# A float32 attention and two-layer chain on one core: the seven products of the first layer's output in another order, and two operand splits one product later

## The chip, the cores and the metric

One core of one Trainium2 chip runs the whole program in one launch. The metric is the device time of that core in microseconds (us), the median of the runs. TensorE (PE) does the matmuls, and its weight loads (PEld) overlap them; VectorE (DVE), ScalarE (ACT) and GpSimd (POOL) do the elementwise work; SyncE (SP) issues most loads. PE writes its sums into eight PSUM banks of 128 x 512 float32.

## What is computed

Attention over 2 x 8 heads, 768 positions of width 64, with a band mask and a few global keys, gives x, a matrix of 1536 x 512. Then come two gated layers:

```
a, b = x @ w1, x @ w2            # 1536 x 1024
y = ((a * b) @ w3) @ w_out       # 1536 x 512: the first layer's output
a, b = y @ w_a, y @ w_b          # 1536 x 1536
out = (a * b) @ w_out2           # 1536 x 512
```

All is float32 in the reference, so every matmul here is made of three: each operand is split into a high part (rounded for PE by a cast on ACT) and a low part (what is left, by a subtraction on DVE), and low x high, high x low and high x high are added up in one bank.

## The kernel before

**Stages.** Attention runs first, with the weight conversion and the first matmuls of layer one in its gaps. Then the gate a * b of layer one and the folded weight w3 @ w_out are finished, until about 265 us of the span. The stage of this document follows: the product y = gate x folded weight (`y_product`, lines 935 to 1007), from 265.4 to 340.4 us. Then come the products of layer two (`products`), and the output.

**Seven products for eight.** `y_product` multiplies 2 x 2 blocks with a scheme of seven products, numbered 1 to 7, where the left operand (a piece of the folded weight, tiles `wf`, or sums of pieces) and the right operand (a piece of the gate, tiles `gs`, or sums) are added beforehand and the results are combined afterwards. It does so twice: q = 0 for 1024 of the tokens (right operands 512 wide), then q = 1 for the last 512 (256 wide). A product is two halves c = 0, 1 of 128 rows; a half is 12 matmuls (four pieces of three) into one bank. So there are 14 products of 24 matmuls, 336 in all.

**Three pairs of banks.** Products 1, 6, 7 and 4 add up in the pair z, product 2 has the pair x, and products 5 and 3 share the pair m. The running sums in the banks are taken out after each product: by a copy on ACT (`nc.scalar.copy`, line 984, tiles `p` and `u`) or by an add on DVE (line 986). The next product that adds onto the same bank waits for that copy or add. The order before is 1, 2, 6, 7, 5, 3, 4:

```
for k in (1, 2, 6, 7, 5, 3, 4):
    ...
    bank = (x if k == 2 else m if k in (5, 3) else z)[c]
```

**What comes of the sums.** The finished sums are y's operands for layer two; each is split by `operand` (ACT cast at line 730, then DVE subtraction at line 731, tiles `y`). After products 2 and 5 this is emitted at once, behind the copies and adds of that product.

**The order of ACT's and DVE's work.** It is what the code emits. The generator `y_steps` (lines 791 to 924) emits the splits of the left and right operands (`left`: ACT line 808, DVE line 809; `right`: ACT line 730, DVE line 731), the sums of gate blocks, made by DMAs that add on the way (`adds`, line 796, issued by POOL), and the preparation of layer two's first weights (`weights` and `wab_steps`, where POOL adds at line 763 into `sf`). `y_product` takes one step of this generator ahead of each product (`next(prepare, None)`). Each engine works through its own queue in this order, so an instruction that waits holds up everything behind it.

Of the kernel before, what the change touches and what calls it, by code (L numbers as in the profile page):

```python
# [31 lines left out]
class Emitter:  # L32
# [758 lines left out]
    def y_steps(self, gu):  # L791
# [22 lines left out]
        def right(q, k, j, src, place=self.unit):  # L814
            if q == 0:
                hi, lo = (place("gs", [P, 2, TG], F32R) for _ in range(2))
                self.yb[0].setdefault(k, []).extend((hi[:, e], lo[:, e]) for e in range(2))
            else:
                if j == 0:
                    self.yb[1][k] = [place("gs", [P, 4, H], F32R) for _ in range(2)]  # L820
                hi, lo = (t[:, 2 * j : 2 * j + 2] for t in self.yb[1][k])
            self.split(hi, lo, src)
            if q and j:
                hi, lo = self.yb[1][k]
                self.yb[1][k] = [(hi[:, e], lo[:, e]) for e in range(4)]

        def rights(q, k, src, place=self.unit):
            for j in range(2):
                right(q, k, j, src[j], place)

        def adds(out, a):
            for j in range(2):
                add(out[j], a[j])

        def weights(f, n):
            if f not in joins:
                self.wab_load(f)
                joins[f] = self.wab_join(f)
            for _ in range(n):
                next(joins[f], None)  # L840
# [34 lines left out]
        yield  # L875
        right(0, 6, 0, t2[0])
        weights(1, 4)
        yield
        right(0, 6, 1, t2[1])
        right(0, 7, 0, b12[0])  # L880
        weights(1, 3)
        yield
        right(0, 7, 1, b12[1])
        left(5, a21)
        steps = self.wab_steps(0)
        yield
        rights(0, 5, b11)
        yield
        left(3, a12)
        rights(0, 3, b22)  # L890
        yield
        left(4, a22)
        rights(0, 4, b21)
        rights(1, 1, c11, self.late)
        adds(c11, c12)
        yield
        adds(c12, c22)
        rights(1, 5, c11)
        adds(c11, c22)
        for _ in range(3):  # L900
            next(steps, None)
        yield
        rights(1, 2, c21, self.late)
        adds(c21, c11)
        for _ in range(2):
            next(steps, None)
        yield
        rights(1, 6, c11)
        for _ in range(2):
            next(steps, None)  # L910
        yield
        rights(1, 7, c12, self.late)
        for _ in range(2):
            next(steps, None)
        yield
        rights(1, 3, c22)
        for _ in range(2):
            next(steps, None)
        yield
        rights(1, 4, c21)  # L920
        yield
# [13 lines left out]
    def y_product(self, prepare):  # L935
# [28 lines left out]
        for q, N in enumerate((TG, TG // 2)):  # L964
            place = (lambda n: self.half(n, [P, 2, N])) if q else (lambda n: self.unit(n, [P, 2, N]))
            z, x, m = [None] * 2, [None] * 2, [None] * 2
            sums = {}
            for k in (1, 2, 6, 7, 5, 3, 4):
                to = {1: "p1", 2: "p1", 6: "u2", 3: "u2", 7: "u3", 5: "u3", 4: "u2"}[k]
                if to not in sums:  # L970
                    sums[to] = place(to)
                t = sums[to]
                next(prepare, None)
                hi, lo = self.ya[k]
                right = self.yb[q].pop(k)
                for c in range(2):
                    if k in (1, 2, 5):
                        {1: z, 2: x, 5: m}[k][c] = self.bank("y", (P, N))
                    bank = (x if k == 2 else m if k in (5, 3) else z)[c]
                    at = slice(c * P, (c + 1) * P)  # L980
                    left = [(hi[:, f, at], lo[:, f, at]) for f in range(4)]
                    self.multiply(bank, left, right, k in (1, 2, 5), True, k in (6, 7, 3, 4))
                    if k in (1, 6, 7):
                        nc.scalar.copy(out=t[:, c], in_=bank)  # L984
                    elif k in (2, 5, 3):
                        nc.vector.tensor_tensor(out=t[:, c], in0=bank, in1=t[:, c], op=ALU.add)
                    else:
                        operand(q, 2, bank, c)
                        sub(t[:, c], bank, sums["u3"][:, c])
                    yield 2.6  # L990
                if k in (2, 5):
                    operand(q, {2: 1, 5: 3}[k], t)
                elif k == 3:
                    p1, u3 = sums["p1"], sums["u3"]
                    sub(p1, t, p1)
                    sub(t, u3, t)
                    operand(q, 7, t)
                    sub(u3, u3, p1)
                if q:
                    next(later, None)  # L1000
            for _ in later:
                pass
            later = last_operands(q, *(sums[n] for n in ("p1", "u2", "u3")))
# [280 lines left out]
```

## Time and profile before

| what | value |
|---|---|
| median of 3 runs | 622.42 us (619.44 to 622.64) |
| the profiled execution: its own time | 622.17 us |
| its span, first to last instruction | 620.4 us |
| PE busy | 592.1 us (95%) |
| DVE busy | 422.3 us (68%) |
| ACT busy | 346.7 us (56%) |
| POOL busy | 136.0 us (22%) |
| mean granted TensorE clock | 0.988 of full |

The span lies 1.8 us below the profiled execution's time, which is itself 0.25 us below the median. Busy shares are means over stages that differ, so the rows further down are taken from the one stage that the change touches.

### The profile page before, as it was taken

The page shows a single profiled execution, that of the slowest core. Times are in us where ns is not written, and L with a number is a line of the kernel's source. Part 1 is how long each engine was busy: PE and PEld are TensorE (multiplying, and loading weights), DVE is VectorE, ACT ScalarE, POOL GpSimd, SP SyncE. Part 2 cuts the span into 40 slices and gives each one's busy share as a digit, 9 for nine tenths or more (in the row PEclk, how much of TensorE's full clock was granted, in tenths as well). Part 3 has the DMA queues.
Part 4 walks back from the last instruction along what each step waited for, and adds up shares of the span by engine and source line. Part 5 has one row for each costly group of instructions (what it writes and reads, how often), then busy time and mean ns, then how long its engine had stood idle before and what let it go on. Part 6 is the DMA issues. An engine that isn't in the chain of part 4 may idle for free.

```text
span 620.4 us, 9681 instructions
## 1 busy us (share of the span) xinstructions
PE 592.1 (95%) x3452; PEld 506.9 (82%) x3452; DVE 422.3 (68%) x912; ACT 346.7 (56%) x747; POOL 136.0 (22%) x190
## 2 busy tenths in 40 slices
PE   6898999999999999998869999999999999999996
PEld 4677988888888888886769888888888888888886
DVE  6988899369864863666885777766677768778100
ACT  6998899657563654466263455544444444555400
POOL 5755767300000002310621022222222210000000
PEclk9999999999999999998987999999999999999999
DMA  8999772335242423990721222222220243030301
GB/s 237 274 263 213 181 195 69 137 116 188 71 149 94 141 92 68 207 200 1 101 35 53 83 69 69 68 69 69 69 68 2 69 136 137 34 102 1 136 35 38
DMA packets 24184, 67.29 MB, mean 108 GB/s; under 512 B 3008, under 2 KB 5824, under 8 KB 24128
## 3 DMA queue, kind: packets, MB, share of 16 engines
q1 hardware_dynamic: 19648, 57.42, 30.5%
q0 software_dynamic: 3904, 8.39, 7.8%
q10 hardware_dynamic: 576, 0.79, 0.5%
q8 instruction: 29, 0.48, 0.3%
q14 instruction: 27, 0.22, 0.1%
HBM read 55.05 MB, written 3.15 MB: 94 GB/s over the span
## 4 chain that ended last, share of the span: by engine, by line
PE 76%; DVE 9%; issue 7%; ACT 3%; DMA 2%; POOL 1%; POOLq 0%; DVEq 0%; ACTq 0%
PE ab_band L930 27%; PE o_band L930 15%; PE ab_band L669 6%; PE ab_band L671 6%; PE ab_band L670 6%; PE y_band L930 3%; PE wfp_band L245 2%; PE wfp_band L243 2%; PE wfp_band L244 2%; PE pv_band L516 2%; PE pt_band L480 2%; DVE s_band L444 2%; DMA qd_band<-in_kq_dram 1%; ACT gs_band L730 1%; DMA g_band<-g_band 1%
## 5 line engine op out<-in xcount | busy, mean ns | idle before, releaser
L930 PE MATMUL ab_band<-y_band,ws_band 128*128 128x512 f32 (+1 forms) x576 | 110.1, 337 | 0.0
L930 PEld LDWEIGHTS ab_band<-y_band,ws_band 128*128 128x128 f32 x576 | 91.0, 190 | 12.0
L930 PE MATMUL o_band<-wo_band,gs_band 128*128 128x512 f32 (+1 forms) x468 | 98.9, 373 | 0.3 <-DVE gs_band L1040 0.3
L930 PEld LDWEIGHTS o_band<-wo_band,gs_band 128*128 128x128 f32 x468 | 83.0, 188 | 16.1 <-DVE gs_band L1040 0.7
L669 PE MATMUL ab_band<-xh_band,w_band 128*128 128x512 f32 (+1 forms) x216 | 81.8, 379 | 0.0
L671 PE MATMUL ab_band<-xh_band,w_band 128*128 128x512 f32 (+1 forms) x216 | 79.0, 366 | 0.0
L670 PE MATMUL ab_band<-xl_band,w_band 128*128 128x512 f32 (+1 forms) x216 | 79.0, 366 | 0.0
L930 PE MATMUL y_band<-gs_band,wf_band 128*128 128x512 f32 (+1 forms) x336 | 65.2, 360 | 10.0 <-ACT u_band L984 6.3
L930 PEld LDWEIGHTS y_band<-gs_band,wf_band 128*128 128x128 f32 x336 | 57.1, 211 | 18.2 <-ACT u_band L984 6.9
L469 POOL TENSOR_SCALAR s_band<-s_band,z_band 128x256 f32<-128x256 f32 (+1 forms) x96 | 61.0, 647 | 35.4 <-DVE z_band L467 14.9
L930 PE MATMUL ab_band<-y_band,wa_band 128*128 128x512 f32 (+1 forms) x288 | 56.4, 338 | 0.0
L90 ACT ACTIVATE raw_band<-raw_band 128x512 int32<-128x512 uint32 x76 | 51.1, 672 | 0.0
L930 PEld LDWEIGHTS ab_band<-y_band,wa_band 128*128 128x128 f32 x288 | 46.0, 190 | 6.1
L456 ACT ACTIVATE s_band<-s_band,m_band 128x256 f32<-128x256 f32 (+1 forms) x96 | 46.7, 495 | 3.5 <-DVE m_band L444 3.4
L678 DVE TENSOR_TENSOR g_band<-ab_band,b_band 128x512 f32<-128x512 f32 (+1 forms) x27 | 16.9, 628 | 45.3 <-ACT b_band L677 45.3
L669 PEld LDWEIGHTS ab_band<-xh_band,w_band 128*128 128x128 f32 x216 | 40.7, 188 | 7.5 <-issue 1.0
L671 PEld LDWEIGHTS ab_band<-xh_band,w_band 128*128 128x128 f32 x216 | 40.6, 188 | 6.7
L670 PEld LDWEIGHTS ab_band<-xl_band,w_band 128*128 128x128 f32 x216 | 40.7, 189 | 6.1
L1079 ACT COPY p_band<-ab_band 128x512 f32<-128x512 f32 (+1 forms) x48 | 22.0, 482 | 38.7 <-PE ab_band L930 38.6
L102 DVE CUSTOM_DVE_ANT_0 g_band<-raw_band,g_band 128x1024 uint16<-128x1024 uint16 x52 | 36.2, 697 | 6.5
L1080 DVE TENSOR_TENSOR u_band<-ab_band,u_band 128x512 f32<-128x512 f32 (+1 forms) x24 | 13.3, 554 | 38.1 <-PE ab_band L930 38.1
L444 DVE CUSTOM_DVE_ANT_0 s_band<-sp_band,bias_band 128x256 f32<-128x256 f32 (+1 forms) x96 | 37.1, 388 | 0.5 <-ACT bias_band L309 0.4
(133 smaller groups left out, 1066.3 us busy)
## 6 DMA issues: line engine op xcount, KB each, us to landing
raw_band<-in_moe_w_dram SPq DMA_DIRECT2D x31, 512.0 KB, 4.7
raw_band<-in_moe_w_out_dram SPq DMA_DIRECT2D x20, 512.0 KB, 3.3
raw_band<-in_moe_w_b_dram SPq DMA_DIRECT2D x12, 512.0 KB, 3.4
raw_band<-in_moe_w_a_dram SPq DMA_DIRECT2D x12, 512.0 KB, 4.1
v_band<-in_v_dram SPq DMA_DIRECT2D x12, 256.0 KB, 8.0
kd_band<-in_kq_dram SPq DMA_DIRECT2D x12, 256.0 KB, 6.8
qd_band<-in_kq_dram SPq DMA_DIRECT2D x12, 256.0 KB, 6.9
out_dram<-o_band SPq DMA_DIRECT2D x11, 256.0 KB, 2.3
```

The costliest lines, as they stand in the source:

```text
L90: nc.scalar.activation(out=low, in_=low.bitcast(U32), func=AF.Copy, scale=2.0**-29)
L102: nc.vector.tensor_tensor(out=gi, in0=gi, in1=low, op=ALU.add)
L444: nc.vector.tensor_tensor_reduce(out=s[:, j, lo:], in0=sp[:, j, lo:], in1=bias[:, 2 * c + j, :], scale=-self.scale, scalar=FLT_MAX, op0=AL ...
L456: nc.scalar.activation(out=s[:, j, lo:], in_=s[:, j, lo:], func=AF.Exp, bias=m[:, j : j + 1], scale=-1.0, accum_out=z[:, j : j + 1],)
L469: nc.gpsimd.tensor_scalar(out=s[:, j, lo:], in0=s[:, j, lo:], scalar1=z[:, j : j + 1], scalar2=1.0, op0=ALU.mult, op1=ALU.mult)
L669: nc.tensor.matmul(p, wl, xh, start=(c == 0), stop=False)
L670: nc.tensor.matmul(p, wh, xl, start=False, stop=False)
L671: nc.tensor.matmul(p, wh, xh, start=False, stop=(c == self.C - 1))
L678: nc.vector.tensor_tensor(out=out[:, at], in0=ps[0], in1=b, op=ALU.mult)
L930: self.nc.tensor.matmul(bank, wt, xt, start=start and i == n == 0, stop=stop and n == 2 and i == len(terms) - 1, skip_group_check=more,)
L1079: copy = lambda out: nc.scalar.copy(out=out, in_=bank)
L1080: plus = lambda t: nc.vector.tensor_tensor(out=t, in0=bank, in1=t, op=ALU.add)
```

## The change

Three things change. The loop's order becomes 1, 2, 6, 5, 7, 3, 4, so that every product adds onto another pair of banks than the product ahead of it. With it the sum `u3`, to which both 7 and 5 contribute, is now copied out after 5 (on ACT) and added to after 7 (on DVE), the other way round than before. The split of y's operands 1 and 3 is put on a list (`behind`) and emitted after the next product's copies or adds. And the steps of `y_steps` are put in another order, so that the operands of product 5 come earlier and those of the second round (tiles of `rights(1, ...)`) are spread; the preparation of the second layer's weights begins later.

```diff
@@ -875,47 +875,45 @@
         right(0, 6, 0, t2[0])
         weights(1, 4)
-        yield
+        left(5, a21)
+        yield
+        right(0, 5, 0, b11[0])
         right(0, 6, 1, t2[1])
+        weights(1, 3)
+        yield
+        right(0, 5, 1, b11[1])
         right(0, 7, 0, b12[0])
-        weights(1, 3)
+        rights(1, 1, c11)
+        adds(c11, c12)
         yield
         right(0, 7, 1, b12[1])
-        left(5, a21)
+        left(3, a12)
+        right(0, 3, 0, b22[0])
+        yield
+        right(0, 3, 1, b22[1])
+        rights(1, 5, c11, self.late)
+        adds(c11, c22)
+        adds(c12, c22)
...
@@ -964,9 +962,9 @@
-            sums = {}
-            for k in (1, 2, 6, 7, 5, 3, 4):
-                to = {1: "p1", 2: "p1", 6: "u2", 3: "u2", 7: "u3", 5: "u3", 4: "u2"}[k]
+            sums, behind = {}, []
+            for k in (1, 2, 6, 5, 7, 3, 4):
+                to = {1: "p1", 2: "p1", 6: "u2", 3: "u2", 5: "u3", 7: "u3", 4: "u2"}[k]
@@ -980,17 +978,18 @@
-                    if k in (1, 6, 7):
+                    if k in (1, 6, 5):
                         nc.scalar.copy(out=t[:, c], in_=bank)
-                    elif k in (2, 5, 3):
+                    elif k in (2, 7, 3):
                         nc.vector.tensor_tensor(out=t[:, c], in0=bank, in1=t[:, c], op=ALU.add)
                     else:
                         operand(q, 2, bank, c)
                         sub(t[:, c], bank, sums["u3"][:, c])
                     yield 2.6
-                if k in (2, 5):
-                    operand(q, {2: 1, 5: 3}[k], t)
-                elif k == 3:
+                for k1, t1 in behind:
+                    operand(q, k1, t1)
+                behind = [({2: 1, 7: 3}[k], t)] if k in (2, 7) else []
+                if k == 3:
```

**ACT around product 6 of the first round.** Before (`p` and `u` copies of line 984 take sums out of the banks `y_band_3284` and `y_band_3298`, the pair z; `y_band_3348` is y's operand 1):

```order
L984 COPY p_band_3273<-y_band_3298 128x512
L730 CAST gs_band_3312<-g_band_2101 128x1024
L808 ACTIVATE wf_band_3316<-wq_band_2579 128x1024
L730 CAST y_band_3348<-p_band_3273 128x1024
L730 CAST gs_band_3353<-g_band_688 128x1024
L730 CAST gs_band_3357<-g_band_933 128x1024
L984 COPY u_band_3352<-y_band_3284 128x512
L984 COPY u_band_3352<-y_band_3298 128x512
L808 ACTIVATE wf_band_3388<-wq_band_2886 128x1024
```

Now (`y_band_3288` and `y_band_3302` are the pair z, `y_band_3418` and `y_band_3432` the pair m, `y_band_3399` is operand 1, and `g_band_2225` and `g_band_2359` are gate blocks of the second round, to which POOL's DMAs add):

```order
L730 CAST gs_band_3369<-g_band_2472 128x1024
L982 COPY u_band_3360<-y_band_3288 128x512
L982 COPY u_band_3360<-y_band_3302 128x512
L730 CAST y_band_3399<-p_band_3277 128x1024
L730 CAST gs_band_3404<-g_band_3058 128x1024
L730 CAST gs_band_3408<-g_band_2225 128x512
L730 CAST gs_band_3408<-g_band_2359 128x512
L982 COPY u_band_3403<-y_band_3418 128x512
L982 COPY u_band_3403<-y_band_3432 128x512
```

The cast of operand 1 stood ahead of product 6's copies and stands behind them now; the copies of product 5 stand behind two casts of gate blocks of the second round.

**ACT around product 6 of the second round.** Before (`y_band_3651` is operand 1, `y_band_3585` and `y_band_3599` the pair z):

```order
L984 COPY p_band_3576<-y_band_3599 128x256
L730 CAST y_band_3613<-u_band_3387 128x1024
L730 CAST gs_band_3617<-g_band_2225 128x512
L730 CAST gs_band_3617<-g_band_2359 128x512
L730 CAST y_band_3651<-p_band_3576 128x512
L730 CAST y_band_3654<-p_band_3273 128x1024
L730 CAST gs_band_3659<-g_band_2503 128x512
L730 CAST gs_band_3659<-g_band_3107 128x512
L984 COPY u_band_3658<-y_band_3585 128x256
L984 COPY u_band_3658<-y_band_3599 128x256
```

Now (`y_band_3693` is operand 1, `y_band_3702` and `y_band_3716` the pair m):

```order
L779 CAST ws_band_3586<-sf_band_3498 128x512
L730 CAST y_band_3656<-p_band_3277 128x1024
L730 CAST gs_band_3661<-g_band_2503 128x512
L730 CAST gs_band_3661<-g_band_3107 128x512
L982 COPY u_band_3660<-y_band_3589 128x256
L982 COPY u_band_3660<-y_band_3603 128x256
L730 CAST y_band_3693<-p_band_3584 128x512
L730 CAST y_band_3696<-u_band_3360 128x1024
L982 COPY u_band_3700<-y_band_3702 128x256
L982 COPY u_band_3700<-y_band_3716 128x256
```

Operand 1 has moved from ahead of product 6's copies to behind them, ahead of product 5's.

**POOL: the adds into the gate blocks of the second round and the sums of layer two's weights.** The difference; `sf` is the weights' sums:

```order
 L796 DMA g_band_2359<-g_band_3107 128x2x256
-L763 TENSOR_TENSOR sf_band_3488<-gb_band_3099 128x256
-L763 TENSOR_TENSOR sf_band_3488<-ga_band_3100,gb_band_3099 128x256
-L763 TENSOR_TENSOR sf_band_3488<-sf_band_3488,ga_band_3100 128x256
-L763 TENSOR_TENSOR sf_band_3488<-ga_band_3100,sf_band_3488 128x256
 L796 DMA g_band_2503<-g_band_2225 128x2x256
 L796 DMA g_band_3107<-g_band_2359 128x2x256
+L763 TENSOR_TENSOR sf_band_3498<-gb_band_3099 128x256
+L763 TENSOR_TENSOR sf_band_3498<-ga_band_3100,gb_band_3099 128x256
+L763 TENSOR_TENSOR sf_band_3498<-sf_band_3498,ga_band_3100 128x256
+L763 TENSOR_TENSOR sf_band_3498<-ga_band_3100,sf_band_3498 128x256
```

All eight DMA issues now stand ahead of the four weight sums.

## Rows read from the trace of the kernel before

**Rows 1.** The page's costliest groups: busy, mean ns | idle before, releaser.

```profile
L930 PE MATMUL y_band<-gs_band,wf_band 128*128 128x512 f32 (+1 forms) x336 | 65.2, 360 | 10.0 <-ACT u_band L984 6.3
```

**Rows 2.** Timeline of PE: start us, us, instructions [idle before <-releaser].

```profile
265.37 16.48 PE L930 MATMUL y_band<-gs_band,wf_band 128*128 128x512 f32 x72
284.19 12.76 PE L930 MATMUL y_band<-gs_band,wf_band 128*128 128x512 f32 x48 [2.35 <-ACT u_band L984]
298.58 14.13 PE L930 MATMUL y_band<-gs_band,wf_band 128*128 128x512 f32 x73 [1.62 <-DVE u_band L986]
314.81 7.38 PE L930 MATMUL y_band<-gs_band,wf_band 128*128 128x256 f32 x47 [2.10 <-DVE gs_band L731]
326.12 14.47 PE L930 MATMUL y_band<-gs_band,wf_band 128*128 128x256 f32 x96 [3.93 <-ACT u_band L984]
340.42 1.55 PE L930 MATMUL ab_band<-y_band,wa_band 128*128 128x512 f32 x6
...
347.25 0.88 PE L930 MATMUL ab_band<-y_band,wa_band 128*128 128x256 f32 x6
347.96 0.28 PE L930 MATMUL ab_band<-y_band,ws_band 128*128 128x256 f32 x1
```

**Rows 3.** Stretches behind each stop: busy (x) of PE, PEld, DVE, ACT, POOL, granted clock, DMA share.

```profile
284.19:287.00 2.81, 2.81 (x7) 2.26 (x8) 2.50 (x3) 2.81 (x4) 0.00 (x0) 0.55 0.00 0
...
298.60:302.00 3.40, 3.40 (x15) 2.83 (x16) 1.65 (x2) 1.63 (x2) 1.68 (x3) 1.00 0.89 127
...
314.80:318.00 3.20, 3.19 (x16) 3.19 (x17) 3.20 (x6) 3.20 (x7) 2.44 (x2) 0.57 0.48 64
...
326.10:328.00 1.90, 1.88 (x9) 1.88 (x10) 1.80 (x3) 1.90 (x4) 0.00 (x0) 0.50 0.00 0
```

**Rows 4.** Timeline of ACT, ahead of the first stop's end.

```profile
280.72 1.05 ACT L730 CAST y_band<-p_band 128x1024 fp32r<-128x1024 f32 x1 [5.12 <-DVE p_band L986]
281.68 1.98 ACT L730 CAST gs_band<-g_band 128x1024 fp32r<-128x1024 f32 x2
283.57 1.06 ACT L984 COPY u_band<-y_band 128x512 f32<-128x512 f32 x2
```

**Rows 5.** Timeline of DVE, ahead of the first and of the second stop.

```profile
279.41 1.28 DVE L986 TENSOR_TENSOR p_band<-y_band,p_band 128x512 f32<-128x512 f32 x2
...
294.27 3.56 DVE L731 TENSOR_TENSOR gs_band<-g_band,gs_band 128x1024 fp32r<-128x1024 f32 x4
297.75 1.28 DVE L986 TENSOR_TENSOR u_band<-y_band,u_band 128x512 f32<-128x512 f32 x2
```

**Rows 6.** Timeline of ACT, ahead of the third and of the fourth stop.

```profile
310.62 1.05 ACT L730 CAST y_band<-u_band 128x1024 fp32r<-128x1024 f32 x1 [6.08 <-DVE u_band L943]
...
323.19 1.56 ACT L730 CAST y_band<-p_band 128x512 fp32r<-128x512 f32 x2 [4.91 <-DVE p_band L986]
```

**Rows 7.** The stage's stretch, columns as in the third group: DVE's busy time is the third.

```profile
265.37:340.42 75.05, 65.05 (x337) 56.95 (x336) 54.51 (x69) 39.41 (x62) 19.13 (x18) 0.91 0.40 69
```

**Rows 8.** Timelines at the stage's start: ACT's cast of a sum made by DMA, DVE's split.

```profile
270.72 1.05 ACT L730 CAST gs_band<-kq 128x1024 fp32r<-128x1024 f32 x1 [0.49 <-DMA kq<-g_band]
...
270.27 1.23 DVE L731 TENSOR_TENSOR gs_band<-kq,gs_band 128x1024 fp32r<-128x1024 f32 x1 [0.24 <-ACT gs_band L730]
```

**Rows 9.** DMA issues of line 796: time to landing, and the issues of half size.

```profile
DMA to landing us min/median/max: 3.8/6.1/15.0
...
g_band<-g_band POOLq DMA_DIRECT2D x8, 256.0 KB, 4.8
```

**Rows 10.** Timelines of DVE and POOL where both work, and alone.

```profile
307.14 1.71 DVE L943 TENSOR_TENSOR p_band<-u_band,p_band 128x1024 f32<-128x1024 f32 x1
...
312.94 1.21 DVE L943 TENSOR_TENSOR u_band<-u_band,p_band 128x1024 f32<-128x1024 f32 x1
...
307.84 3.27 POOL L763 TENSOR_TENSOR sf_band<-sf_band,ga_band 128x256 f32<-128x256 f32 x1
...
333.15 0.73 POOL L763 TENSOR_TENSOR sf_band<-sf_band,ga_band 128x256 f32<-128x256 f32 x1
```

More of the change, by code (lines that the diff above doesn't have):

```diff
@@ L877, in y_steps @@
         weights(1, 4)
+        left(5, a21)
         yield
+        right(0, 5, 0, b11[0])
         right(0, 6, 1, t2[1])
-        right(0, 7, 0, b12[0])
         weights(1, 3)
         yield
-        right(0, 7, 1, b12[1])
-        left(5, a21)
+        right(0, 5, 1, b11[1])
+        right(0, 7, 0, b12[0])
+        rights(1, 1, c11)
+        adds(c11, c12)
+        yield
+        right(0, 7, 1, b12[1])
+        left(3, a12)
[6 more added lines that the diff above has]
+        yield
+        left(4, a22)
+        right(0, 4, 0, b21[0])
+        rights(1, 2, c21)
+        adds(c21, c11)
         steps = self.wab_steps(0)
         yield
-        rights(0, 5, b11)
-        yield
[L889 to L907, printed above, removed]
+        right(0, 4, 1, b21[1])
         rights(1, 6, c11)
-        for _ in range(2):
-            next(steps, None)
+        next(steps)
         yield
         rights(1, 7, c12, self.late)
+        next(steps)
+        next(steps)
+        yield
         for _ in range(2):
@@ L916, in y_steps @@
         rights(1, 3, c22)
-        for _ in range(2):
-            next(steps, None)
+        next(steps)
         yield
```

## The prediction

> **What bounds the kernel now.** I read the page first, then PE's timeline in the stage, then the granted clock behind each stop, then the queues of ACT and DVE ahead of each stop. The page puts 10.0 us of idle time before the matmuls of this stage and names ACT's copy of a sum as the main releaser [rows 1]. PE's timeline shows where: the 14 products run from 265.37 to 340.42, 75.05 us, with four stops, 2.35 + 1.62 + 2.10 + 3.93 = 10.0 us [rows 2]. Outside these stops PE always has work here, and the page's PE is busy for 592.1 of 620.4 us, so a microsecond of the stage is one of the total.
>
> The stops cost more than their length. Behind the stops of 2.35, 2.10 and 3.93 us the granted clock is 0.55, 0.57 and 0.50, the lower of the two levels, 1.2 GHz; behind the stop of 1.62 us it stays at 1.00 [rows 3]. What that costs comes from the starts. At full clock a 512-wide matmul takes 0.227 us (72 of them in 16.48 less a tail of 0.16), a 256-wide one 0.118 (six in 347.96 - 347.25 = 0.71) [rows 2]. The 48 behind the first stop need 298.58 - 1.62 - 284.19 = 12.8 us against 48 x 0.227 = 10.9: 1.9 lost. The 47 behind the third need 326.12 - 3.93 - 314.81 = 7.4 against 5.5: 1.8 lost. The 96 behind the fourth need 14.3 against 11.3: 3.0 lost. Together 6.7 us of slow clock.
>
> Why the stops are there: the first and the fourth are product 7 waiting for z, whose copy after product 6 is late. ACT is free much earlier, but the next thing in its queue is the cast of operand 1, which waits 5.12 us for DVE's add; only behind it and two more casts does the copy run, at 283.57 [rows 4]. The fourth is the same, with 4.91 us of waiting [rows 6]. In the second stop product 3 waits for m, and DVE's add stands behind four operand splits that end at 297.8 [rows 5]. The third is a late operand: DVE splits the piece late because ACT stood 6.08 us before an operand cast [rows 6], and DVE behind it.
>
> **The change, part by part.** The matmuls are the same 336, in another order, and ACT, DVE and POOL do the same work in another order; nothing is added or removed. With no stop and full clock the stage takes 168 x 0.227 + 168 x 0.118 = 38.1 + 19.8 = 57.9 us. That is 75.05 - 57.9 = 17.1 us less (10.0 of stops, 6.7 of clock, 0.4 of tails). What has to be worked out is whether each wait fits into the new time table. Halves of the first round start every 2.72 us: product 1 at 265.4, 2 at 270.8, 6 at 276.3, 5 at 281.7, 7 at 287.1, 3 at 292.6, 4 at 298.0. The second round starts at 303.5 with halves of 1.42: product 6 at 309.1, 5 at 312.0, 7 at 314.8, 3 at 317.6, 4 at 320.5, end at 323.3. I walk the two queues with what back-to-back work takes: four DVE splits, two wide and two half as wide, take 3.56 [rows 5], so 1.15 and 0.6; ACT's two wide casts take 1.98 and its two copies 1.06 [rows 4], starts 0.95 and 0.48 apart.
>
> First round. *Product 6, operand t2[1]:* ACT's cast of this sum waits for the DMA until 270.72 now [rows 8]; it was free from 270.2, and two casts moved ahead of it put it at 272.1 to 273.1. DVE starts the low part of t2[0] at 270.27 [rows 8], then four small steps of the weights (2.1), two wide splits that moved ahead of it, and is through with t2[1] at 277.0. The seventh matmul of product 6 is the first to need it, near 277.8: 0.8 us to spare. *Product 7 onto z* needs the copies after 6: ACT comes to them at 279.7, and 7 starts at 287.1: 7 us to spare, since product 5 now lies between. *Product 3 onto m* needs the copies after 5. These stand behind the cast of operand 1 (DVE's adds are done at 283.0) and two casts of c11, a sum that POOL's DMAs make; POOL can issue them when DVE has split c11, near 281.8, and such a half-size DMA lands 4.8 us later [rows 9]: the copies end at 288.2, 3 starts at 292.6, 4 us to spare. *Product 4 onto z* needs DVE's adds after 7. DVE is busy without a gap from 277 on (0.7 + 0.6 for the weights, nine wide splits 10.3, eight half-size steps 4.8) and comes to them at 293.4: 4 us to spare.
>
> Second round. DVE goes on with four wide and six half-size steps, one of which waits for product 3's end at 298.0, and stands at 302.4 when the first two differences are done; ACT's cast of operand 7 costs it 1.2 of waiting, and it ends the adds after product 2 at 314.0. ACT's copies after 6 come at 311.4 (needed 314.8: 2 to 3 us to spare), after 5 at 315.8 to 316.4 (needed 317.6: 1.2), DVE's adds after 7 end at 319.4 (needed 320.5: 1.0). So everything fits, but DVE is what comes next: it has 54.5 us of work in this stretch [rows 7], and the new stretch is 58. The three smallest margins (0.8, 1.2, 1.0) hang on it.
>
> What I add for that: at least 0, since PE can't be quicker than full clock without stops. At most, if DVE falls 3 us behind, 2.2 of stops at the second round's end, 2.2 at product 6 and 1.8 of slow clock [rows 3], some 6. The step with a measured size is POOL's sums for the weights, now at some 295 to 302, where DVE is busy: a difference on DVE took 1.71 beside them and 1.21 alone, and a POOL sum 3.27 beside DVE and 0.73 alone [rows 10]. Two or three such hits are 1 to 1.5 us on DVE, most of it within the margins. I take 0.7, near the lower end, since the margins cover what these rows show. The weight sums themselves may take 10 us there and still be in time: ACT's cast of them comes at 305.6.
>
> The Trainium skill, page "SBUF — State Buffer", section "SBUF: two separate sides", says more: GpSimd and a DVE instruction with two SBUF inputs exclude each other for a whole instruction, whichever starts first. The rows agree in kind: both engines were slower there. By this rule each of the four POOL sums could hold DVE for the whole of its 0.73, 2.9 us in all, which is the second rival below.
>
> Behind the stage nothing moves: layer two's first products wait for operands whose splits keep their distance to the stage's end, and the next weights' loads are issued with it. So the profiled execution would come to 622.17 - 17.1 + 0.7 = 605.8. The median of the runs is 0.25 above that execution: **606.0 us**.
>
> **The rivals.** *Forecast:* margins hold, stops of at most 1 us in all, 605 to 607. For it speaks that every wait of before that ended a stop has 2 us or more in the new order, but for three; chance 0.72.
>
> *DVE as the new bound:* POOL's sums or late DMAs put DVE 2 to 4 us behind. Product 4 of the second round then waits 1 to 3 us, product 6 of the first perhaps too, and with a stop above 2 us the clock falls for another 1.8 [rows 3]: 607 to 611, say 609. For it: 54.5 of 58 us; against it: some DVE work lies ahead of the stage's first wait, and some can come after its end. Chance 0.20.
>
> *ACT held by the DMA sums of the second round (the other side):* the copies after 5 now stand behind casts of c11, and those behind POOL's DMAs. With a landing time L the copies end near 282.9 + L, so product 3 waits when L is above 9.7. The second pair of sums is issued after the first has landed and been split, and holds ACT again, with the casts that free z and the copies of the second round behind it, so each further microsecond of L costs about two, and slow clock with it. At 15 us, the longest landing of any issue of this line [rows 9], I reckon some 10 us of stops and 7 of clock: the whole gain. From some 16.5 us on the kernel is slower by over 3, at 18 us at 628. Against it: DMA was idle ahead of these issues [rows 3], the half-size ones took 4.8, and 15 was seen among twelve issues of full size. Chance 0.02 for slower, 0.03 for a landing of 10 to 13 that leaves 612 to 617.
>
> *The change doesn't do what it says:* the stops come back elsewhere, at the entry to layer two for instance, because ACT and DVE are as late there as before and PE only arrives earlier: 619 to 625, 0.03. Against it: both engines have 5 us or more before their sums of the last products are needed there, before and now.
>
> **How the numbers follow.** Within 0.5% (3.1 us) is about what a measurement of this kernel can tell from no change. Faster: 0.72 + 0.20 + 0.03 = 0.95; same 0.03; slower 0.02. The forecast and most of the second rival make the range: from 603.5 (no stop at all, 605.3 on the median, and 1.8 below it for the runs' own spread, which is 3.2 in the three shown) to 611.
>
> **What would show it.** Right: PE's timeline of the stage in one piece of about 58 us, or with stops below 1.6 us and a clock of 1.00 throughout; copies after 6 on ACT ahead of the cast of operand 1; DVE busy over 85% of the stage. The second rival: a stop released by a DVE split or add in product 6 of the first round or 3 or 4 of the second. The third: casts of gate blocks on ACT waiting for a DMA by more than 5 us. Wrong: a stage of more than 65 us, or idle time of PE in the first 60 us behind it that wasn't there before.

## The result and the profile after

| | before | changed |
|---|---|---|
| median | 622.32 us (619.44 to 622.64, 4 runs) | 606.68 us (605.18 to 607.04, 4 runs) |
| the profiled execution: its own time | 622.17 us | 605.18 us |
| its span | 620.4 us | 603.4 us |
| the stage, first y product to first product of layer two | 75.05 us | 58.23 us |
| stops of PE in the stage | 10.0 us | none |

The ratio is 0.9749, with a 95% interval of 0.9718 to 0.978: faster by 2.5%. 606.0 was forecast, in a range of 603.5 to 611.0.

In the changed kernel the multiplies stand at line 928, the copies at 982, the adds at 984, the differences at 941. The page's group for the matmuls of the stage, which answers to [rows 1]:

```profile
L928 PE MATMUL y_band<-gs_band,wf_band 128*128 128x512 f32 (+1 forms) x336 | 58.4, 336 | 0.0
```

The same 336 matmuls, with no idle time before any of them, where 10.0 us stood. PE's timeline, for [rows 2], is one row for the 14 products and then layer two's first:

```profile
265.23 58.40 PE L928 MATMUL y_band<-gs_band,wf_band 128*128 128x512 f32 x336
323.46 1.55 PE L928 MATMUL ab_band<-y_band,wa_band 128*128 128x512 f32 x6
```

The stretches (columns as in [rows 3]): the whole stage, its two parts, and all that lies behind it.

```profile
265.23:323.46 58.23, 58.23 (x337) 51.70 (x336) 52.89 (x67) 38.57 (x60) 18.39 (x18) 1.00 0.51 90
265.23:300.00 34.77, 34.77 (x155) 28.82 (x154) 31.00 (x37) 26.57 (x38) 14.46 (x14) 1.00 0.77 130
300.00:323.46 23.46, 23.46 (x184) 22.88 (x183) 21.89 (x31) 12.00 (x22) 3.93 (x5) 1.00 0.13 30
323.46:603.40 279.94, 274.76 (x1478) 237.87 (x1476) 176.22 (x301) 126.41 (x229) 33.47 (x40) 1.00 0.21 71
```

The granted clock is 1.00 in all four. DVE's work is nearly as large as before (52.9 us against 54.5 in [rows 7]), but it is now 91% of the stage. The same view of before, from the stage's end on:

```profile
340.42:620.40 279.98, 274.76 (x1478) 237.75 (x1476) 175.39 (x299) 126.01 (x228) 33.47 (x40) 1.00 0.21 71
```

279.98 before and 279.94 now: nothing is given back later. The accounts of the two profiled executions close: 0.14 us ahead of the stage (265.37 against 265.23), 75.05 - 58.23 = 16.82 in it, 0.04 behind it, 17.0 in all, and 622.17 - 605.18 = 16.99.

ACT's timeline around product 6 of the first round, for [rows 4]:

```profile
279.58 0.60 ACT L982 COPY u_band<-y_band 128x512 f32<-128x512 f32 x1
281.75 0.59 ACT L982 COPY u_band<-y_band 128x512 f32<-128x512 f32 x1 [1.57 <-PE y_band L928]
282.93 1.06 ACT L730 CAST y_band<-p_band 128x1024 fp32r<-128x1024 f32 x1 [0.59 <-DVE p_band L984]
283.88 1.05 ACT L730 CAST gs_band<-g_band 128x1024 fp32r<-128x1024 f32 x1
285.27 0.62 ACT L730 CAST gs_band<-g_band 128x512 fp32r<-128x512 f32 x1 [0.33 <-DMA g_band<-g_band]
286.95 0.62 ACT L730 CAST gs_band<-g_band 128x512 fp32r<-128x512 f32 x1 [1.06 <-DMA g_band<-g_band]
287.48 1.07 ACT L982 COPY u_band<-y_band 128x512 f32<-128x512 f32 x2
```

The copies after product 6 stand ahead of operand 1's cast, which waits 0.59 us for DVE's adds where it waited 5.12. The second copy waits for PE itself to end the product. Before, the copies made PE wait ([rows 2], 2.35 us).

And in the second round, ACT and then DVE, for [rows 6] and [rows 5]:

```profile
311.66 0.86 ACT L982 COPY u_band<-y_band 128x256 f32<-128x256 f32 x2
314.78 0.62 ACT L730 CAST y_band<-p_band 128x512 fp32r<-128x512 f32 x1 [2.27 <-DVE p_band L984]
```

```profile
314.00 0.75 DVE L984 TENSOR_TENSOR p_band<-y_band,p_band 128x256 f32<-128x256 f32 x2
...
319.34 1.08 DVE L984 TENSOR_TENSOR u_band<-y_band,u_band 128x256 f32<-128x256 f32 x3
320.78 0.42 DVE L984 TENSOR_TENSOR u_band<-y_band,u_band 128x256 f32<-128x256 f32 x1 [0.36 <-PE y_band L928]
```

The last row is DVE waiting for PE: at the end of the stage DVE has caught up.

### The profile page after: what moved, and what is told of

It reads as the page before. It is cut to its first block, busy times and chain, and to the rows that moved or that the text cites. A ratio compares the mean times of both kernels' runs of the same rounds, so it can differ in the third digit from the quotient of the medians.

```text
span 603.4 us, 9696 instructions
## 1 busy us (share of the span) xinstructions
PE 585.0 (97%) x3452; PEld 501.9 (83%) x3452; DVE 421.3 (70%) x912; ACT 346.2 (57%) x747; POOL 135.7 (22%) x190
## 4 chain that ended last, share of the span: by engine, by line
PE 86%; DVE 7%; ACT 2%; issue 2%; DMA 1%; POOL 0%; SPq 0%; DVEq 0%; ACTq 0%
PE ab_band L928 28%; PE o_band L928 15%; PE y_band L928 10%; PE ab_band L669 7%; PE ab_band L670 6%; PE ab_band L671 6%; PE wfp_band L243 2%; PE wfp_band L244 2%; PE wfp_band L245 2%; PE pv_band L516 2%; PE pt_band L480 2%; PE sp_band L410 2%; DVE s_band L444 2%; DMA kq<-in_kq_dram 1%; DVE qb_band L383 1%
## 5 line engine op out<-in xcount | busy, mean ns | idle before, releaser
L469 POOL TENSOR_SCALAR s_band<-s_band,z_band 128x256 f32<-128x256 f32 (+1 forms) x96 | 62.9, 667 | 34.3 <-DVE z_band L467 14.1
L928 PE MATMUL y_band<-gs_band,wf_band 128*128 128x512 f32 (+1 forms) x336 | 58.4, 336 | 0.0
L928 PEld LDWEIGHTS y_band<-gs_band,wf_band 128*128 128x128 f32 x336 | 51.8, 190 | 6.6
L1079 DVE TENSOR_TENSOR u_band<-ab_band,u_band 128x512 f32<-128x512 f32 (+1 forms) x24 | 13.3, 555 | 38.1 <-PE ab_band L928 38.1
```

Source lines behind the costliest of these rows:

```text
L469: nc.gpsimd.tensor_scalar(out=s[:, j, lo:], in0=s[:, j, lo:], scalar1=z[:, j : j + 1], scalar2=1.0, op0=ALU.mult, op1=ALU.mult)
L928: self.nc.tensor.matmul(bank, wt, xt, start=start and i == n == 0, stop=stop and n == 2 and i == len(terms) - 1, skip_group_check=more,)
L1079: plus = lambda t: nc.vector.tensor_tensor(out=t, in0=bank, in1=t, op=ALU.add)
```

## The experiments

**What was to be told apart.** My theory: three separate causes made the four stops (the reuse of a bank at once, copies queued behind an operand's cast, one late operand), each part of the change removes one, and the clock and the gain come back only when all are gone. One rival: the order of banks, which names the change, does nearly all. Another: the later split does. And a question on what is left: how near to new stops the changed kernel is, that is, how much cover each wait has (how much later the work may come before PE waits for it).

**The change in parts.** O is the order alone, with the roles of 5 and 7 that go with it:

```diff
-            for k in (1, 2, 6, 7, 5, 3, 4):
+            for k in (1, 2, 6, 5, 7, 3, 4):
...
-                    if k in (1, 6, 7):
+                    if k in (1, 6, 5):
                         nc.scalar.copy(out=t[:, c], in_=bank)
-                    elif k in (2, 5, 3):
+                    elif k in (2, 7, 3):
...
-                if k in (2, 5):
-                    operand(q, {2: 1, 5: 3}[k], t)
+                if k in (2, 7):
+                    operand(q, {2: 1, 7: 3}[k], t)
```

> The loop's new order alone; operands 1 and 3 are split at once as before, and the steps of the operands stand as before. My theory (a stop ends when the late piece of ACT's or DVE's queue fits behind the product, and all three parts are needed for that): product 5 now lies between 6 and 7, so the copies after 6 have 5.4 us more and the stop of 3.93 in the second round goes; but 5's operands come later than PE now wants them, and c11 and c21 stay late, so some 4 to 6 us of stops are left (products 5 and 7 of the first round, 2 and 5 to 3 of the second), the clock falls once: 612 to 616. Rival 1 (the bank order does it all): no stop, 606 to 607. Rival 2 (the later split of the operands does it): the stops of 2.35 and 3.93 stay, 620 to 623.

B is the later split alone, in the old order:

```diff
-            sums = {}
+            sums, behind = {}, []
...
-                if k in (2, 5):
-                    operand(q, {2: 1, 5: 3}[k], t)
-                elif k == 3:
+                for k1, t1 in behind:
+                    operand(q, k1, t1)
+                behind = [({2: 1, 5: 3}[k], t)] if k in (2, 5) else []
+                if k == 3:
```

> The later split of operands 1 and 3 alone, in the old order 6, 7, 5 and with the old steps. My theory: the copies after 6 are no longer behind a cast that waits for DVE, so the first stop (2.35) goes and the one of 3.93 shrinks to about 1, while those of 1.62 and 2.10, which DVE's queue makes, stay or move: some 4 us of stops, one or two falls of the clock, 611 to 616. Rival 1 (bank order does it all): as before, 621 to 623. Rival 2 (the later split does it all): 606 to 608.

S is the new `y_steps` (the first hunk of the change) with the loop of before:

> The new order of the operand steps alone, with the loop and the splits as before. My theory: nothing of the late copies is mended and ACT's queue is fuller ahead of them, so the first stop grows to about 5 and the one of 3.93 stays, while the third (2.10, the late operand c21) goes: 10 to 11 us of stops and the clock's share: 622 to 626, no faster than before. Rivals 1 and 2: 621 to 623. A third rival (it is the supply of operands that counts): 606 to 612.

Then the pairs: O with B, O with S, B with S, each by the diffs above put together.

> The new order and the later split, with the old steps: the change without its table of steps. My theory: the stops at z and m are gone, but c11 is split and summed as late as before, so product 2 of the second round waits for its right operand for 2 to 4 us in all, the clock falls once: 610 to 614. Rivals 1 and 2: 606 to 607, since the steps do nothing.

> The new order and the new steps, but operands 1 and 3 split at once as before. My theory: the first round runs without a stop (product 5 gives the copies after 6 room enough), but in the second round the cast of operand 1 stands ahead of ACT's copies again, where a product half is only 1.42 us and DVE is late: a stop of 4 to 6 us there at product 7 or 5 to 3, and the clock falls for 3 more: 613 to 617. A theory in which order and steps do it and the later split adds nothing: 606 to 607.

> The later split and the new steps, in the old order 6, 7, 5, 3. My theory: the copies after 6 are in time, but 7 now comes a product before the place for which its operands were put in the new steps, and two products in a row still share a pair of banks, so short stops are left at 7 and 3 of the first round (0.4 to 1 each) and one of 2 to 3 in the second round, where product 3 or 4 waits for DVE's adds: 3 to 4.5 us of stops, 609 to 613. If the order adds nothing: 606 to 607. If the order is what counts: 615 or more.

And the changed kernel once more, beside the last two pairs on the same chip:

> The changed kernel once more, beside the others on the same chip: 605 to 607.5 by every theory; its profile says whether a stop or a fall of the clock comes and goes from run to run (the profiled execution was 1.5 us faster than the median).

The ratios are to the runs of before in the same set (median 621.8 us for O, B, S and O + B, 622.2 for the last three); the row of before is that of the result.

| kernel | median us | ratio to before, 95% | stage us | stops, us (who released PE) |
|---|---|---|---|---|
| before | 622.3 | | 75.05 | 2.35 ACT copy, 1.62 DVE add, 2.10 DVE split, 3.93 ACT copy |
| O | 617.39 | 0.9905 to 0.9951 | 69.18 | 0.94 ACT cast, 0.95 DVE split, 1.52 ACT cast, 2.15 DVE split, 1.05 ACT copy |
| B | 614.8 | 0.9877 to 0.991 | 66.68 | 1.62 DVE add, 1.32 ACT cast, 2.10 DVE split |
| S | 623.28 | 1.0009 to 1.0039 | 74.76 | 5.71 ACT copy, 0.40 DVE add, 5.81 ACT copy |
| O + B | 613.81 | 0.9854 to 0.9894 | 65.56 | 3.19 ACT cast, 1.89 DVE split |
| O + S | 615.21 | 0.9871 to 0.9904 | 66.52 | 0.28 ACT copy, 0.69 DVE split, 4.66 ACT copy |
| B + S | 609.54 | 0.9778 to 0.9811 | 61.71 | 0.83 DVE split, 0.40 DVE add, 1.39 DVE add |
| all, again | 606.23 | 0.972 to 0.9753 | 58.24 | none |

Three readings. PE's timeline of S alone:

```profile
288.85 12.57 PE L928 MATMUL y_band<-gs_band,wf_band 128*128 128x512 f32 x48 [5.71 <-ACT u_band L982]
301.81 19.82 PE L928 MATMUL y_band<-gs_band,wf_band 128*128 128x512 f32 x120 [0.40 <-DVE u_band L984]
327.45 14.13 PE L928 MATMUL y_band<-gs_band,wf_band 128*128 128x256 f32 x96 [5.81 <-ACT u_band L982]
```

The late operand of the second round, which stopped product 2 for 2.10, is gone, and product 3's stop, for which DVE's adds stood behind four operand splits, is down from 1.62 to 0.40. But the two copies of product 6 come later still. ACT's timeline of the same kernel says why:

```profile
284.43 1.04 ACT L730 CAST y_band<-p_band 128x1024 fp32r<-128x1024 f32 x1 [6.13 <-DVE p_band L984]
285.38 1.04 ACT L730 CAST gs_band<-g_band 128x1024 fp32r<-128x1024 f32 x1
286.33 1.05 ACT L808 ACTIVATE wf_band<-wq_band 128x1024 fp32r<-128x1024 f32 x1
287.29 1.03 ACT L730 CAST gs_band<-g_band 128x1024 fp32r<-128x1024 f32 x1
288.22 1.06 ACT L982 COPY u_band<-y_band 128x512 f32<-128x512 f32 x2
```

Operand 1's cast is still ahead of the copies, DVE's adds come later than before, and the cast holds ACT for 6.13 us instead of 5.12.

PE's timeline of B alone is the reverse: product 7's two stops are gone, and what stays is the bank m and the late operand, which now stops PE twice, for ACT's cast and then for DVE's low part.

```profile
294.82 14.01 PE L930 MATMUL y_band<-gs_band,wf_band 128*128 128x512 f32 x72 [1.62 <-DVE u_band L986]
310.15 0.38 PE L930 MATMUL y_band<-gs_band,wf_band 128*128 128x256 f32 x1 [1.32 <-ACT gs_band L730]
312.63 20.04 PE L930 MATMUL y_band<-gs_band,wf_band 128*128 128x256 f32 x143 [2.10 <-DVE gs_band L731]
```

And O alone ends product 3's wait for m and product 7's in the first round, and cuts product 7's in the second from 3.93 to 1.05, but product 5 now wants its operand a product earlier than the old steps deliver it (0.94 and 0.95), and the late operand of the second round stays:

```profile
283.80 0.50 PE L930 MATMUL y_band<-gs_band,wf_band 128*128 128x512 f32 x1 [0.94 <-ACT gs_band L730]
285.25 26.19 PE L930 MATMUL y_band<-gs_band,wf_band 128*128 128x512 f32 x119 [0.95 <-DVE gs_band L731]
...
315.49 10.26 PE L930 MATMUL y_band<-gs_band,wf_band 128*128 128x256 f32 x71 [2.15 <-DVE gs_band L731]
326.81 8.90 PE L930 MATMUL y_band<-gs_band,wf_band 128*128 128x256 f32 x72 [1.05 <-ACT u_band L984]
```

O was expected at 612 to 616 and came at 617.4. Most of the places were named, product 5 among them, but the size was missed: the stops are 6.6 us in all where 4 to 6 were expected, and the clock fell twice and not once. The other five medians of the series fell into what the theory said.

So the late operand needs S: every kernel without S keeps it, none with S has it. The bank m needs O, and S takes most of it. Product 7's stop in the second round needs B: O leaves 1.05 of it and O + S 4.66. In the first round O or B is enough against it (O + S leaves 0.28), but O alone brings product 5 ahead of its operands, and either of the other two mends that. With B added to O the whole first round runs in one piece:

```profile
266.17 41.19 PE L930 MATMUL y_band<-gs_band,wf_band 128*128 128x512 f32 x192
```

Both rivals fall: O alone gives 5.9 us of the stage, B alone 8.4, S alone 0.3, a sum of 14.5, where the three together give 16.8. The last part added is worth 3.5 (O to B + S), 8.3 (B to O + S) or 7.3 us (S to O + B). The order named in the change is the smallest of the three as a last step: without it three stops stay, 2.62 us in all, with the clock at 1.00 behind each; the other 0.9 us are not in these stops (three tails of 0.16, the end of the last matmul ahead of a stop, are half of them). S alone is even 1.5 us slower by its median (623.28 against 621.8), though its stage is 0.3 shorter; its profiled execution reached the stage at 266.66, 1.3 later than that of before. That lies ahead of all that the steps touch; from 20 to 60 us of the span its granted clock was 0.96, where that of before was 1.00. Whether the median's 1.5 us come from there in all ten runs, one trace can't show.

**How near the next stop is.** Extra work on a scratch tile, put into DVE's or ACT's queue of the changed kernel. First DVE, behind its adds after product 7 of the first round:

```diff
+                for _ in range(8 if (q, k) == (0, 7) else 0):
+                    nc.vector.tensor_tensor(out=self.pad, in0=self.pad, in1=self.pad, op=ALU.mult)
                 for k1, t1 in behind:
```

> The changed kernel with eight multiplications of a scratch tile (128 x 384) on DVE behind the add after product 7 of the first round, some 0.46 us each and 3.7 in all, that nobody reads. My theory (DVE is the next bound, with about 1 us to spare in the second round): PE gets stops of 2.5 to 3.5 us in all, in products 6 to 4 of the second round; if one is above 2 us the clock falls too: 609 to 612. Rival (DVE has several us to spare, it was the releaser only by the order of its queue): 606 to 607.5, no stop.

It came at 613.21 us (ratio 0.9832 to 0.9868): a miss. The load was twice as long as thought, 7.88 us for 3.7, and it met a wait that I had not listed. DVE's timeline, and the group of its line (ns, least, median, most):

```profile
295.33 7.88 DVE L990 TENSOR_TENSOR pad<-pad 128x384 f32<-128x384 f32 x8
```

```profile
L990 DVE TENSOR_TENSOR pad<-pad x8: 548/558/3334, 295.3 to 302.7; 128x384 f32<-128x384 f32 x8
```

One of the eight took 3334 ns where the median is 558. It lies beside POOL's sums (in DVE's stretches one multiply alone is at work from 297.5 to 300). From POOL's timeline:

```profile
297.41 1.22 POOL L763 TENSOR_TENSOR sf_band<-gb_band 128x256 f32<-128x256 f32 x1
298.11 1.21 POOL L763 TENSOR_TENSOR sf_band<-ga_band,gb_band 128x256 f32<-128x256 f32 x1
298.81 1.20 POOL L763 TENSOR_TENSOR sf_band<-sf_band,ga_band 128x256 f32<-128x256 f32 x1
300.09 0.93 POOL L763 TENSOR_TENSOR sf_band<-ga_band,sf_band 128x256 f32<-128x256 f32 x1
```

And the stop is at product 4 of the first round, not in the second:

```profile
304.41 27.00 PE L928 MATMUL y_band<-gs_band,wf_band 128*128 128x512 f32 x185 [3.82 <-DVE gs_band L731]
```

Seven matmuls of product 4 run, and the eighth waits for an operand which DVE splits behind the load. 7.88 of load make 3.82 of stop: some 4 us of cover for that operand. Behind the stop the clock was 0.50 until 310, and the stage took 65.05, 6.8 more: 3.8 of stop and 3.0 of slow clock.

Then DVE in the second round, at a place where no sum of POOL's runs: the same lines with `(q, k) == (1, 2)`, three and eight times.

> The changed kernel with three extra multiplies of 128 x 384 on VectorE (a scratch tile, no product's data) behind the adds after product 2 of the second round, where no GpSimd sum runs. Some 0.55 us each, 1.6 us in all. Theory that VectorE's margin there is the 0.85 us between the first add after product 7 (done near 319.7 in the changed kernel) and product 4's start at 320.5: one stop of 0.6 to 0.9 us at product 4, released by VectorE, no fall of the clock, 606.8 to 607.8. Rival, that VectorE has slack in that round which the walk of the queue missed: no stop, 605.9 to 606.8.

> The same with eight multiplies, some 4.3 us in the same place. Theory: the first add after product 7 comes near 324, so one stop of 3 to 4 us at product 4 of the second round, released by VectorE, and the granted clock at the lower level behind it, 1.5 to 3 us: 610.5 to 613.5. Rival (slack that the walk missed): a stop under 2 us and no fall of the clock, 607 to 609.

606.95 us (0.9744 to 0.9779) and 611.6 us (0.9813 to 0.9863), both as the theory had them. PE's timeline with three, then with eight, and the stretch behind the second stop:

```profile
322.64 3.13 PE L928 MATMUL y_band<-gs_band,wf_band 128*128 128x256 f32 x24 [0.73 <-DVE u_band L984]
```

```profile
326.04 4.64 PE L928 MATMUL y_band<-gs_band,wf_band 128*128 128x256 f32 x24 [3.68 <-DVE u_band L984]
```

```profile
326.04:328.00 1.96, 1.96 (x9) 1.96 (x10) 1.94 (x5) 0.62 (x1) 1.96 (x3) 0.53 0.22 82
```

With three, DVE's adds after product 7 began 1.66 us later against the stage's start than in the changed kernel (322.17 - 266.40 against 319.34 - 265.23); with eight, 4.61 (325.57 - 266.85). Less the stops, that leaves 0.93 us of cover both times, counted to the first of the two adds, the one that product 4 waits for.

Last ACT, ahead of its copies after product 5 of the first round, seven and fourteen times:

```diff
+                    for _ in range(7 if (q, k, c) == (0, 5, 0) else 0):
+                        nc.scalar.copy(out=self.pad, in_=self.pad)
                     if k in (1, 6, 5):
                         nc.scalar.copy(out=t[:, c], in_=bank)
```

> The changed kernel with seven extra copies of 128 x 384 on ScalarE (a scratch tile) ahead of its copies after product 5 of the first round, as if the sums by DMA ahead of them had landed 3 us later. Theory (margins as walked: 4 us at product 3, 4 us at product 4, with some 2 us of waits in VectorE's queue that swallow most of a delay before the second round): no stop above 0.5 us, 605.9 to 607.5. Rival, the third one of the prediction, that ScalarE's queue has no such slack and each microsecond there costs about two: 610 to 613.

> The same with fourteen copies, some 5.8 us, as if the landing time were 12 to 13 us. Theory: the copies after product 5 end near 294 where product 3 wants the first at 292.6: a stop of 1 to 1.5 us at product 3, released by ScalarE, and 1 to 2 us of stops by late VectorE work at product 4 or in the second round; 608 to 611. The third rival's price for such a landing was 612 to 617, by a chain of delays through the second pair of sums and slow clock.

609.1 us (0.9777 to 0.9815) and 612.4 us (0.9832 to 0.9873): both misses for the theory's numbers. The extra copies started 0.53 us apart, so the delays were 3.7 and 7.5 us, and a place was missing from my list. PE's timeline with seven (copies are at line 984 here):

```profile
311.81 8.89 PE L928 MATMUL y_band<-gs_band,wf_band 128*128 128x256 f32 x72 [1.15 <-ACT p_band L984]
321.42 6.28 PE L928 MATMUL y_band<-gs_band,wf_band 128*128 128x256 f32 x48 [0.71 <-ACT u_band L984]
```

Product 3 of the first round holds. The stops are at products 6 and 3 of the second round: the copies after product 1 stand on ACT behind a cast that waits for DVE's difference, and that came late, since DVE waited 3.45 us for a cast of ACT's:

```profile
294.63 1.22 DVE L809 SCALAR_TENSOR_TENSOR wf_band<-wq_band,wf_band 128x1024 fp32r<-128x1024 f32 x1 [3.45 <-ACT wf_band L808]
```

I had counted on waits in DVE's queue to swallow this. They didn't: the wait of 1.17 for ACT's cast moved along with the rest, and three splits ahead of product 3's adds took 3.63 us where they take 2.42 in the changed kernel, now beside POOL's first two sums (from 299.48 on):

```profile
299.31 3.63 DVE L731 TENSOR_TENSOR gs_band<-g_band,gs_band 128x1024 fp32r<-128x1024 f32 x3
```

With fourteen:

```profile
295.74 34.50 PE L928 MATMUL y_band<-gs_band,wf_band 128*128 128x512 f32 x216 [3.00 <-ACT u_band L984]
```

```profile
298.00:301.00 3.00, 3.00 (x8) 2.31 (x7) 3.00 (x5) 3.00 (x7) 0.57 (x1) 0.50 0.00 0
```

One stop, at product 3: 7.5 - 3.0 = 4.5 us of cover, and slow clock for about 3.3 us more. The later stops don't come, since PE itself is now 6.3 us late: ACT's copies after product 1 come 7.1 us later than in the changed kernel, which the 2 us of cover that they have there make good. 612.4 is the lower end of the third rival's price for such a landing, 612 to 617. But the copies delay less than a late landing would: they stand behind the casts of the first pair of sums, and POOL issued the second pair as early as in the changed kernel (24.2 us after the stage's start in both).

## Why the prediction was right

**The four stops and their cost.** Right as put. All four went, with their clock and tails: 16.82 us in the stage where 17.1 less 0.7 was forecast. That there is more than one cause is shown by the parts: no part alone and no pair ends all the stops, and the late operand, the bank m and product 7's stop in the second round each need another part.

**What the stage takes without stops.** 57.9 forecast, 58.23 measured. The 512-wide matmuls fit: with fourteen copies on ACT the first 120 of them ran without a break in 27.36 us, less a tail of 0.16, 0.227 each. So the 168 narrow ones took (58.23 - 38.1) / 168 = 0.120 and not the 0.118 that six of them gave [rows 2]: 0.3 us more in the sum.

**The residual of 0.7 for DVE.** Measured 0: no stop at all. DVE was delayed beside POOL's sums (296.4 to 300.7), but the margins covered it:

```profile
298.68 1.46 DVE L731 TENSOR_TENSOR y_band<-u_band,y_band 128x1024 fp32r<-128x1024 f32 x1
300.06 1.75 DVE L941 TENSOR_TENSOR p_band<-u_band,p_band 128x1024 f32<-128x1024 f32 x1
301.85 1.23 DVE L941 TENSOR_TENSOR u_band<-u_band,u_band 128x1024 f32<-128x1024 f32 x1
```

The first two take 1.22 elsewhere: 0.8 us of hits, which I had put at 1 to 1.5. DVE stood at 303.1 behind the second difference where I had 302.4, and was still 0.7 late when its adds after product 7 ended, at 320.1 for 319.4.

**The margins.** The walk through the queues was right to within 0.8 us:

| event | forecast | measured |
|---|---|---|
| product 6's t2[1] split | 277.0 | 276.9 |
| ACT's copies after 6 begin | 279.7 | 279.58 |
| copies after 5 end | 288.2 | 288.55 |
| DVE's adds after 7 begin | 293.4 | 293.16 |
| second round: copies after 6 begin | 311.4 | 311.66 |
| adds after 2 end | 314.0 | 314.75 |
| copies after 5 begin | 315.8 | 316.27 |
| adds after 7 end | 319.4 | 320.1 |

The cover at product 3 of the first round was put at 4 and measured as 4.5. That at product 4 of the second was put at 1.0 and measured as 0.93, which is partly luck: the adds came 0.7 us later than I had them, but I had counted to the end of both adds, and product 4 waits for the first. The 4 us that I had for product 4 of the first round are those ahead of its bank; no run tested them, and the some 4 that the eight multiplies found there belong to its operand. That wait was missing from the list, and so was another: product 6 of the second round waits for ACT's copies after product 1. They began at 306.63 and are wanted at 309.1, some 2 us of cover, and this was the first to give way when ACT was delayed.

**The rivals.** DVE didn't become the bound, but it is what comes next: 91% busy, and only 0.93 us of delay behind product 2 of the second round are free. The hold by POOL's sums that I feared exists, but it cost little here. The Trainium skill, page "SBUF — State Buffer", section "SBUF: two separate sides", says that a GpSimd instruction that reads SBUF and a DVE instruction with two SBUF inputs exclude each other for a whole instruction. By that rule I had put 4 x 0.73 = 2.9 us on the four sums; with eight multiplies on DVE one of them, with two SBUF inputs and beside these sums, took 3334 - 558 = 2776 ns more than its fellows. So the trace agrees that it was held out; that it lasted through three sums in a row and not one goes beyond what the rule says. In the changed kernel itself DVE adds out of the banks or stands idle until 298.7, through most of the first three sums, and the two rows above are the 0.8 us that the sums cost it.

The landing of the half-size sums was 5.4 us by the page's median; ACT waited 0.33 and 1.06 us for the first pair. I had put about two us, and slow clock with it, on each microsecond of landing beyond product 3's cover. Fourteen copies go 7.5 - 4.5 = 3.0 us beyond it and cost 5.95 us against 606.45, the mean of the changed kernel's two medians: two for one, but as one of stop and one of slow clock behind it. Seven copies stay inside that cover, and their 3.7 us cost 2.65 by the wait that was missing from my list. The second hold on ACT, by a late second pair of sums, was in neither run, so the price of a landing that is really late stays open.

**The median.** 606.0 was forecast and 606.68 measured, and that this is so near is partly luck. The sum was made for the profiled execution, 605.8, and came to 605.18: the 0.7 that didn't come outweighs the 0.3 of the narrow matmuls. The step that was off by more is the last, 0.25 us from there to the median. It was 1.5 in the first set, and the second set's median lay 0.64 below its profile. The second profiled execution, 606.87 us, has the same stage (58.24) but began it at 266.88.

## What to carry to other kernels

Where an accumulator is taken out by an engine that also casts operands, look at what stands ahead of the copy in that engine's queue, not at how busy the engine is: ACT was 56% busy over the kernel and ended two of the four stops. Stops with separate causes hide behind each other, so test a change of several parts by its pairs as well as its single parts: here the steps are worth 0.3 us alone and 7.3 as the last part. And once PE runs in one piece, ask each queue for its cover at each wait; extra instructions on a scratch tile measure it, if their length is read from the trace and not assumed: three and eight multiplies gave the same 0.93 us, but eight at another place took 7.88 us for 3.7.

## What the runs showed that I had not expected

**The clock behind short stops.** In these traces it was 0.50 to 0.62 behind the stops of 2.10 us and more, and 1.00 behind single stops of up to 1.62. But with O alone it also fell behind two stops of 0.94 and 0.95 us that had one matmul between them:

```profile
285.25:288.00 2.75, 2.75 (x7) 2.17 (x8) 2.43 (x3) 2.75 (x4) 0.00 (x0) 0.50 0.00 0
```

**Start of the stage.** Between two executions of the same changed kernel 1.65 us lie ahead of the stage (265.23 and 266.88). In the second the granted clock from 20 to 60 us of the span was 0.96, in the first 1.00. Over the 14 traces of all kernels the two go together only roughly: at 1.00 the stage starts at 265.19 to 266.07 (six traces), at 0.93 to 0.97 at 266.17 to 266.88 (eight), but the 0.93 (three multiplies in the second round) starts at 266.40 and 0.96 up to half a microsecond later. So a spread of some 1.7 us between executions lies ahead of this stage, and the clock there is at most a part of its cause.

**A long hold from short sums.** Three POOL sums of 1.2 us each, close behind one another (297.41, 298.11, 298.81), stand beside a single DVE multiply that took 2.8 us longer than its fellows: by these rows it did not get in between them, and ended about when the third did. The spans on POOL are rough, and this is one instruction in one trace; with seven copies on ACT three DVE splits beside two sums took 1.2 us longer.
